# One transpose by DMA for the probabilities of two heads, and the loads of the later batches on GpSimd's queue

## The chip, the cores and the metric

The kernel runs on one core of a Trainium2 chip. The metric is the device time of one execution in microseconds, the median of several runs. The engines are TensorE (PE), VectorE (DVE), ScalarE (ACT), GpSimd (POOL) and SyncE (SP), which here does nothing but issue DMAs; 16 DMA engines move the data for whoever issues.

## The reference

Attention over 4 batches, 12 heads, 448 positions and 64 columns a head, with q and k normalized by rows; its output, 1792 tokens of 768 columns, goes through two expert layers with inner width 2048. All in f32.

```python
q_n, k_n = rmsnorm(q, g_q), rmsnorm(k, g_k)
scores = np.matmul(q_n, k_n.transpose(0, 1, 3, 2)) / np.sqrt(64)
attn = np.exp(scores - scores.max(-1, keepdims=True))
attn = attn / (attn.sum(-1, keepdims=True) + 1e-09)
x = np.matmul(attn, v).transpose(0, 2, 1, 3).reshape(1792, 768)
h = x @ moe_w_in                          # 768 x 2048
y = (h / (1 + np.exp(-1.702 * h))) @ moe_w_out
h = y @ moe2_w_in
out = (np.maximum(h, 0) + moe2_alpha * np.minimum(h, 0)) @ moe2_w_out
```

## The kernel before

**Numbers.** Most factors are split into a high and a low part of 16 bits, and a product is three matmuls (high by high, high by low, low by high) into one f32 sum. To split well, each operand is first scaled by a power of two taken from its largest entry, so that the largest entry of a batch's v has to be known before the batch's v can be split.

**Work.** Heads go in pairs: 24 pairs, six a batch, and a pair has four units: three of 128 rows of both heads and one of 64 rows of both heads, the two heads of which share the 128 partitions. Batch 0 is done in f32 and transposes on PE. For batches 1 to 3 a pair passes through these steps:

- `load_qk` (lines 353 to 356) and `load_v` (368 to 371): four loads for k and q, three for v. There are three buffers for q and k and two for v.
- `normalize`: squares (ACT, line 395), row sums (DVE, 397), reciprocal roots by a seed and three rounds (POOL, 398 to 408, 14 short instructions for two pairs), then the gains and the roots (417, 418). For pairs 8 to 11, the last four of batch 1, POOL also does 417, 418 and the subtraction at 452; otherwise DVE does.
- `prep_pair`: the split of q and k (451, 452), one transpose by DMA of the whole pair (454, a source of 128 x 1792 in f16), the split of v and two copies within SBUF (459, 460).
- for each unit: `scores` (PE, 499; row maxima on DVE, 504, ACT, 506), `exponent` (ACT, 523), `high` (565) and `low` (DVE, 592), which split the normalized probabilities, and the transposes by DMA of line 598, one for each head.
- `values` (PE, 616): the transposed probabilities by v, once for every two units.

`v_scale(b)` finds the largest entry of a batch's v ahead of time: eight pieces of the batch's v are loaded one after another into two buffers (310) and reduced on DVE (311).

**Order.** Attention of batch b+1 is woven into the first expert layer of batch b (`first_moe1`, then `moe1`: lines 720, 767 and 790). The order of the instructions on each engine is planned at build time: an instruction takes the next free slot of its engine on a simulated time line once its inputs and its buffer are there, and the order of the program decides only between those that are ready. So a load without inputs may stand far ahead of its place in the program. Some loads are held back by hand: `tc.issue_after(ins)` lets the instructions of its block that run on the engine of `ins` follow `ins`. It is used for the pieces of v of batch 1 (behind the last load of the first layer's first weights), of batches 2 and 3 (behind the q-and-k transpose of the last pair but one of the batch before), and for the first pairs of batch 1 (behind a load of the first layer's second weights). All three name an instruction of SP. Each engine then works through its list in order; SP issues every DMA of the kernel, and a DMA that must wait for a buffer or for data holds what follows it on SP.

After attention of batch 3 the rest of the first layer and the whole second layer follow (lines 892 and 1052), almost all on PE.

Of the kernel before, what the change touches and what calls it, by code (L numbers as in the profile page):

```python
# [10 lines left out]
F16 = mybir.dt.float16  # L11
# [45 lines left out]
def attention_moe_kernel(  # L57
# [17 lines left out]
    nc = tc.nc  # L75
    B, H, S, D = q.shape
# [60 lines left out]
    def split(dst, src, scale):  # L137

        nc.scalar.activation(out=dst[0], in_=src, func=AF.Copy, scale=scale)  # L139
        nc.vector.scalar_tensor_tensor(  # L140
            out=dst[1], in0=src, scalar=scale, in1=dst[0], op0=ALU.mult, op1=ALU.subtract
        )
# [124 lines left out]
    att_p = att.enter_context(tc.tile_pool(name="att_p", bufs=2))  # L267
# [29 lines left out]
    def v_scales(b, col):  # L297
        one = small.tile([128, 1], F32, tag="vone", name="vone")
        nc.vector.tensor_reduce(out=one, in_=col, op=ALU.max, axis=AX)
        pow2floor(one, one)  # L300
        partition_max(mv[:, b:b + 1], one)
        scaled_reciprocal(av[:, b:b + 1], mv[:, b:b + 1], 2.0 ** 13)

    def v_scale(b):
        flat = v[b].rearrange("h s d -> (h s d)").rearrange("(p n) -> p n", p=128)
        n = flat.shape[1] // VN
        col = small.tile([128, VN], F32, tag="vcol", name="vcol")
        for i in range(VN):
            t = raw_p.tile([128, n], F32, tag="vst", name="vst")
            nc.sync.dma_start(out=t, in_=flat[:, i * n:(i + 1) * n])  # L310
            nc.vector.tensor_reduce(out=col[:, i:i + 1], in_=t, op=ALU.max, axis=AX, apply_absolute_value=True)
        v_scales(b, col)

# [5 lines left out]
    def first_tiles(P):  # L319

        if P < 4:
            part = held[:, HOLD + P * HELD:]
            a = 2 * NT2 * 128
            return (
                part[:, 0:a].bitcast(F32).rearrange("p (i t) -> p i t", t=S),
                part[:, a:HELD].bitcast(F32).rearrange("p (h c d) -> p h c d", h=2, d=D)
            )
        vr = att_p.tile([128, 22 * D], F16, tag="vs", name="v0")
        return (
            att_p.tile([128, 2, S], F32, tag="t1", name="t1"),  # L330
            vr[:, 0:4 * NV * D].bitcast(F32).rearrange("p (h c d) -> p h c d", h=2, d=D)
        )

    HELD = 2 * NT2 * 128 + 4 * NV * D
    ST = S - S % 128


    def main_rows(src, b, p):

        return src[b, 2 * p:2 * p + 2, 0:ST].rearrange("h (p c) d -> p h (c d)", c=3)  # L340

    def some_rows(src, b, p, first, step=1):

        return src[b, 2 * p:2 * p + 2, first:first + 64 * step:step].rearrange("h s d -> s h d")

    def load_qk(P):

        if P >= B * NP:
            return
        b, p = divmod(P, NP)  # L350
        qk = raw_p.tile([128, 2, NT2, D], F32, tag="qk", name="qk", bufs=QKB)
        places = qk.rearrange("p h c d -> p h (c d)")
        nc.sync.dma_start(out=places[:, :, 0:3 * D], in_=main_rows(k, b, p))
        nc.sync.dma_start(out=places[:, :, 4 * D:], in_=main_rows(q, b, p))
        nc.sync.dma_start(out=qk[0:64, :, 3], in_=some_rows(k, b, p, ST))
        nc.sync.dma_start(out=qk[64:128, :, 3], in_=some_rows(q, b, p, ST))
        raws[P] = qk

    def load_v(P):
        if P >= B * NP:  # L360
            return
        b, p = divmod(P, NP)
        if b:
            vr = raw_p.tile([128, 2, NV, D], F32, tag="vr", name="vr")
        else:
            firsts[P] = first_tiles(P)
            vr = firsts[P][1]
        nc.sync.dma_start(out=vr.rearrange("p h c d -> p h (c d)")[:, :, 0:3 * D], in_=main_rows(v, b, p))
        h = 0 if b else 64
        nc.sync.dma_start(out=vr[h:h + 64, :, 3], in_=some_rows(v, b, p, ST))  # L370
        nc.sync.dma_start(out=vr[64 - h:128 - h, :, 3], in_=some_rows(v, b, p, 0, 3))
        rawv[P] = vr

    preps = {}
# [90 lines left out]
    pts = {}  # L465
# [10 lines left out]
    def unit(u):  # L476

        P, r = divmod(u, 4)
        return (P, *UNITS[r])
# [88 lines left out]
    def low(u):  # L568
        P, half, cols, place = unit(u)
        if u < 4 * NP:  # L570
            pr, _ = probs.pop(u)
            n = len(pr)
            if (P, half) not in pts:
                pts[P, half] = att_p.tile([128, NV, 512], F32, tag="pt", name="ptf")
            for h in range(2):
                tp = ps_m.tile([128, 2, n, 128], F32, tag="m", name="tp")
                for c in range(2):
                    o = min(128 * (2 * h + c), S - 128)
                    for i in range(n):
                        nc.tensor.transpose(out=tp[:, c, i], in_=pr[i][:, o:o + 128], identity=identf)  # L580
                d = cols[1] - cols[0]
                to = pts[P, half][:, 2 * h:2 * h + 2, 0:2 * d].rearrange("p c (i t) -> p c i t", i=2)
                to = to[:, :, :, cols[0]:cols[0] + 64 * n]
                src = tp if n == 2 else tp.rearrange("p c n (i t) -> p c (n i) t", i=2)
                nc.scalar.activation(out=to, in_=src, func=AF.Copy)
            if u % 2:
                spread_sums(P, half)
            return
        pr, sm, ph = probs.pop(u)
        n = len(pr)  # L590
        for i in range(n):
            nc.vector.scalar_tensor_tensor(  # L592
                out=ph[:, i, S:2 * S], in0=pr[i], scalar=sm[:, i:i + 1], in1=ph[:, i, 0:S], op0=ALU.mult, op1=ALU.subtract
            )
        if (P, half) not in pts:
            pts[P, half] = att_p.tile([128, 7, 512], F16, tag="pt", name="pt")
        for i in range(2):
            nc.sync.dma_start_transpose(  # L598
                out=pts[P, half][:, :, cols[i]:cols[i] + 64 * n], in_=ph[:, i] if n == 2 else ph[64 * i:64 * i + 64, 0]
            )  # L600

    def values(P, half):
        b, p = divmod(P, NP)
        vs = preps[P][1]
        pt = pts.pop((P, half))
        if half == 0 or b == 0:
            xps[P] = ps_x.tile([128, S], F32, tag="x", name="xp")
        xp = xps[P]
        if b == 0:
            steps = [(c, c, slice(64 if c == 3 else 0, 128)) for c in range(NV)]  # L610
        else:
            steps = [(c, c, slice(0, 128)) for c in range(7)] + [(c + 7, c, slice(0, 128)) for c in range(4)]
        parts = PARTS[half]
        for i, (c, kc, ks) in enumerate(steps):
            for j, o, t, n in parts:
                nc.tensor.matmul(  # L616
                    out=xp[64 * j:64 * j + 64, t:t + n],
                    lhsT=vs[ks, j, c],
                    rhs=pt[ks, kc, o:o + n],
                    start=(i == 0),  # L620
                    stop=(i == len(steps) - 1),
                )
        if b and half == 0:
            xs[b, p] = big.tile([128, 2, S], F16, tag="x", name="x", bufs=NX)
        elif b:
            x = xs[b, p]
            split((x[:, 0], x[:, 1]), xp, scales["w1i"][1][:, p:p + 1])
        elif half == 0:
            own = spread.pop((P, 0))
            nc.vector.tensor_tensor(out=own, in0=xp[:, 0:FIRST], in1=own, op=ALU.mult)  # L630
        else:
            own = spread.pop((P, 1))
            cols = slice(FIRST, S)
            nc.vector.scalar_tensor_tensor(
                out=own, in0=xp[:, cols], scalar=first_sc[:, p:p + 1], in1=own, op0=ALU.mult, op1=ALU.mult
            )
            x = xs[0, p]
            nc.scalar.activation(out=x[:, 0, cols], in_=own, func=AF.Copy)
            nc.vector.tensor_tensor(out=x[:, 1, cols], in0=own, in1=x[:, 0, cols], op=ALU.subtract)
# [504 lines left out]
    if True:  # L1144
        make_identity(nc, ident)
        nc.vector.memset(ones, 1.0)
        nc.vector.tensor_copy(out=identf, in_=ident)
        load_qk(0)
        gains()
        load_v(0)  # L1150
        load_qk(1)
        load_v(1)
# [115 lines left out]
```

## Time and profile before

| | us |
|---|---|
| median of 3 runs | 1183.44 (1181.72 to 1184.11) |
| the profiled execution | 1184.74 |
| its span, first to last instruction | 1183.0 |
| PE busy | 1073.3 (91%) |
| DVE busy | 819.6 (69%) |
| ACT busy | 673.3 (57%) |
| POOL busy | 79.7 (7%) |

Busy shares are means over stages with different limits: the start up to 206 us with batch 0 and the splitting of the weights, batches 1 to 3 of attention from 206 to 652 us, and the rest. Issuing DMAs isn't counted as busy time, so that SP has no row; what its queue does is read from the single issues.

### The profile page before, as it was taken

How to read it: one execution, taken by the hardware profiler on the slowest of the kernel's cores; microseconds unless marked ns; L12 is line 12 of the kernel's file. 1: busy time of each engine (PE TensorE's matmuls, PEld its weight loads, DVE VectorE, ACT ScalarE, POOL GpSimd, SP SyncE). 2: the span in 40 equal slices, each digit the busy share in tenths (PEclk: the TensorE clock that was granted, in tenths of full speed). 3: DMA queues.
4: the chain of work that ended last, by engine and by line, in shares of the span. 5: the costliest groups of instructions: out<-in, count | busy, mean ns of one | idle time of the engine just before them, and what ended most of it. 6: DMA issues, size and time to landing. Idle time of an engine off the chain costs nothing.

```text
span 1183.0 us, 18327 instructions
## 1 busy us (share of the span) xinstructions
PE 1073.3 (91%) x6755; PEld 586.6 (50%) x6755; DVE 819.6 (69%) x1445; ACT 673.3 (57%) x1348; POOL 79.7 (7%) x200
## 2 busy tenths in 40 slices
PE   3468799688789989999998999999999999999998
PEld 1234467554344444545454545544444467666665
DVE  6989999986767886467741868489996322978351
ACT  4667776787767875578742545256555423655220
POOL 2300001442011101100000000000000000000000
PEclk9579799899999999999998999999999999999999
DMA  7944542569888685666553821275624423353111
GB/s 232 266 144 137 150 135 77 113 138 182 160 158 157 136 157 121 122 122 115 93 128 65 307 92 52 99 255 178 224 78 144 142 72 123 99 173 101 34 30 31
DMA packets 256458, 158.06 MB, mean 134 GB/s; under 512 B 177648, under 2 KB 239728, under 8 KB 256368
## 3 DMA queue, kind: packets, MB, share of 16 engines
q1 hardware_dynamic: 256368, 156.89, 50.9%
q8 instruction: 53, 0.87, 0.3%
q14 instruction: 37, 0.30, 0.1%
HBM read 92.22 MB, written 25.69 MB: 100 GB/s over the span
## 4 chain that ended last, share of the span: by engine, by line
PE 32%; DVE 20%; DMA 10%; ACT 10%; issue 5%; SPq 3%; POOL 2%; ACTq 0%; POOLq 0%; DVEq 0%
PE op L1052 16%; PE h L892 7%; PE yp L790 5%; ACT pr L523 3%; DVE ph L592 3%; PE hp L767 3%; DVE nm L504 2%; ACT ph L565 2%; SPq L598 2%; DMA yr<-y_dram 2%; DMA qk<-in_q_dram 1%; DMA pt<-ph 1%; DMA t<-hl 1%; DVE g L140 1%; DMA vst<-in_v_dram 1%
## 5 line engine op out<-in xcount | busy, mean ns | idle before, releaser
L790 PE MATMUL yp<-g,w1o 128*128 128x448 f16 x1152 | 228.2, 355 | 1.9 <-DVE g L140 1.6
L892 PE MATMUL h<-x,w2i 128*128 128x512 f16 (+1 forms) x1152 | 218.9, 352 | 2.7 <-DVE pos L898 1.7
L767 PE MATMUL hp<-x,w1i 128*128 128x448 f16 x864 | 172.1, 356 | 3.7 <-DVE t L776 1.8
L892 PEld LDWEIGHTS <-w2i 128*128 128x128 f16 x1152 | 112.6, 98 | 108.1 <-issue 3.5
L790 PEld LDWEIGHTS <-w1o 128*128 128x128 f16 x1152 | 109.8, 98 | 111.8 <-issue 13.2
L767 PEld LDWEIGHTS <-w1i 128*128 128x128 f16 x864 | 82.8, 99 | 88.2 <-issue 15.7
L592 DVE SCALAR_TENSOR_TENSOR ph<-pr,sm,ph 128x448 f16<-128x448 f32 x126 | 86.9, 717 | 20.2 <-ACT ph L565 19.3
L504 DVE TENSOR_REDUCE nm<-sp 128x2 f32<-128x896 f32 x96 | 92.4, 963 | 0.4 <-PE sp L499 0.4
L523 ACT ACTIVATE pr<-sp,nm,c_s 128x448 f32<-128x448 f32 x126 | 90.0, 717 | 2.8 <-DVE ph L592 1.0
L897 ACT ACTIVATE pos<-h,sign 128x512 f32<-128x512 f32 (+1 forms) x64 | 40.2, 629 | 86.0 <-PE h L892 80.2
L565 ACT ACTIVATE ph<-pr,sm 128x448 f16<-128x448 f32 x126 | 77.8, 659 | 18.3 <-DVE sm L562 15.3
L1052 PEld LDWEIGHTS <-even 128*128 128x128 f16 x672 | 65.7, 98 | 43.4
L898 DVE SCALAR_TENSOR_TENSOR pos<-h,slope,pos 128x512 f32<-128x512 f32 (+1 forms) x64 | 43.4, 680 | 57.9 <-ACT pos L897 57.9
L720 PE MATMUL hp<-x,w1i 128*128 128x256 f16 (+1 forms) x576 | 63.9, 273 | 10.0 <-DVE t L732 4.8
L499 PE MATMUL sp<-t 64*128 64x448 f16 (+1 forms) x432 | 56.2, 365 | 17.0 <-ACT pr L523 17.0
L1052 PEld LDWEIGHTS <-odd 128*128 128x128 f16 x504 | 49.3, 98 | 32.6
L616 PE MATMUL xp<-pt,vs 128*64 128x256 f16 (+1 forms) x792 | 50.2, 271 | 16.6 <-DMA pt<-ph 8.4
L1052 PE MATMUL op<-w2lo,even 128*128 128x384 f16 x384 | 63.4, 326 | 0.0
L720 PEld LDWEIGHTS <-w1i 128*128 128x128 f16 x576 | 54.6, 103 | 17.5 <-issue 12.9
L140 DVE SCALAR_TENSOR_TENSOR g<-t,ratio_w1o,g 128x448 f16<-128x448 f32 x64 | 47.0, 736 | 15.0 <-ACT g L139 14.9
L506 ACT ACTIVATE nm<-nm,c_s 128x2 f32<-128x2 f32 x72 | 20.9, 290 | 62.4 <-DVE nm L504 62.2
L616 PEld LDWEIGHTS <-vs 128*64 128x64 f16 x792 | 39.3, 114 | 33.7 <-issue 18.7
(228 smaller groups left out, 1553.8 us busy)
## 6 DMA issues: line engine op xcount, KB each, us to landing
g<-in_moe_w_in_dram SPq DMA_DIRECT2D x24, 512.0 KB, 5.7
g<-in_moe_w_out_dram SPq DMA_DIRECT2D x32, 384.0 KB, 3.7
w2raw<-in_moe_w_in_dram SPq DMA_DIRECT2D x24, 512.0 KB, 5.6
w2raw<-in_moe_w_out_dram SPq DMA_DIRECT2D x16, 768.0 KB, 6.3
g_dram<-pos SPq DMA_DIRECT2D x48, 256.0 KB, 2.0
gp<-g_dram SPq DMA_DIRECT2D x8, 1024.0 KB, 6.7
odd<-g_dram SPq DMA_DIRECT2D x6, 1024.0 KB, 5.4
y_dram<-y SPq DMA_DIRECT2D x24, 224.0 KB, 2.5
```

Source lines behind the costliest of these rows:

```text
L140: nc.vector.scalar_tensor_tensor(out=dst[1], in0=src, scalar=scale, in1=dst[0], op0=ALU.mult, op1=ALU.subtract)
L499: nc.tensor.matmul(out=sp[:, j, 0:S] if n == 2 else sp[ds, 0, 0:S], lhsT=qt[ds] if n == 2 else qt[ds, 64:128], rhs=kt[ds, 0:S], start=(i = ...
L504: nc.vector.tensor_reduce(out=nm[:, 0:n], in_=sp[:, 0:n, 0:S], op=ALU.max, axis=AX, negate=True)
L523: nc.scalar.activation(out=pr[i], in_=sp[:, i, 0:S], func=AF.Exp, bias=nm[:, i:i + 1], scale=c_s if u >= 4 * NP else 1.0, accum_out=sm[:, ...
L565: nc.scalar.activation(out=ph[:, i, 0:S], in_=pr[i], func=AF.Copy, scale=sm[:, i:i + 1])
L592: nc.vector.scalar_tensor_tensor(out=ph[:, i, S:2 * S], in0=pr[i], scalar=sm[:, i:i + 1], in1=ph[:, i, 0:S], op0=ALU.mult, op1=ALU.subtract)
L616: nc.tensor.matmul(out=xp[64 * j:64 * j + 64, t:t + n], lhsT=vs[ks, j, c], rhs=pt[ks, kc, o:o + n], start=(i == 0), stop=(i == len(steps) ...
L720: nc.tensor.matmul(out=ps, lhsT=w1i[:, kk, e, m * 128:(m + 1) * 128], rhs=xs[0, kk][:, f, cols], start=(i == 0), stop=(i == 3 * KD - 1))
L767: nc.tensor.matmul(out=ps, lhsT=w1i[:, kk, e, m * 128:(m + 1) * 128], rhs=x[:, f], start=(n == 0), stop=(n == 3 * KD - 1))
L790: nc.tensor.matmul(out=ps, lhsT=w1o[:, m, e, j * 128:(j + 1) * 128], rhs=g[:, m, f], start=(n == 0), stop=(n == 3 * KF - 1))
L892: nc.tensor.matmul(out=ps, lhsT=w2i[:, kk, e, m * 128:(m + 1) * 128], rhs=x2[kk][:, f], start=(c == 0), stop=(c == 3 * KD - 1))
L1052: nc.tensor.matmul(out=ps, lhsT=ops[:, o, m, f], rhs=rhs[:, e], start=(c == 0), stop=(c == 3 * KH - 1))
```

## The change

Two edits.

The transposed probabilities of a unit, so far 7 blocks of 512 columns with both heads side by side, become 14 blocks of 256 columns, 7 for each head. For the three units with 128 rows of both heads one transpose of 128 x 1792 takes the place of two of 128 x 896. The unit with 64 rows keeps its two. `values` reads the same number of columns from the new places.

The loads of q, k and v of batches 1 to 3, in `load_qk`, `load_v` and `v_scale`, are issued by GpSimd; those of batch 0, and all other DMAs, stay on SyncE. The uses of `issue_after` aren't touched.

```diff
@@ v_scale
-            nc.sync.dma_start(out=t, in_=flat[:, i * n:(i + 1) * n])
+            nc.gpsimd.dma_start(out=t, in_=flat[:, i * n:(i + 1) * n])
@@ load_qk
-        nc.sync.dma_start(out=places[:, :, 0:3 * D], in_=main_rows(k, b, p))
-        nc.sync.dma_start(out=places[:, :, 4 * D:], in_=main_rows(q, b, p))
-        nc.sync.dma_start(out=qk[0:64, :, 3], in_=some_rows(k, b, p, ST))
-        nc.sync.dma_start(out=qk[64:128, :, 3], in_=some_rows(q, b, p, ST))
+        queue = nc.gpsimd if b else nc.sync
+        queue.dma_start(out=places[:, :, 0:3 * D], in_=main_rows(k, b, p))
+        queue.dma_start(out=places[:, :, 4 * D:], in_=main_rows(q, b, p))
+        queue.dma_start(out=qk[0:64, :, 3], in_=some_rows(k, b, p, ST))
+        queue.dma_start(out=qk[64:128, :, 3], in_=some_rows(q, b, p, ST))
@@ load_v (its three loads in the same way)
@@ low
-            pts[P, half] = att_p.tile([128, 7, 512], F16, tag="pt", name="pt")
-        for i in range(2):
+            pts[P, half] = att_p.tile([128, 14, 256], F16, tag="pt", name="pt")
+        pt = pts[P, half]
+        if n == 2:
             nc.sync.dma_start_transpose(
-                out=pts[P, half][:, :, cols[i]:cols[i] + 64 * n], in_=ph[:, i] if n == 2 else ph[64 * i:64 * i + 64, 0]
+                out=pt[:, :, cols[0]:cols[0] + 128], in_=ph.rearrange("p i k -> p (i k)")
             )
+        else:
+            for i in range(2):
+                nc.sync.dma_start_transpose(out=pt[:, 7 * i:7 * i + 7, 128:192], in_=ph[64 * i:64 * i + 64, 0])
@@ values
-                    rhs=pt[ks, kc, o:o + n],
+                    rhs=pt[ks, 7 * j + kc, 0:n] if b else pt[ks, kc, o:o + n],
```

## Rows read from the trace of the kernel before

**Rows 1.** Stages: stretch, length, busy of the engines, PE clock, DMA share, GB/s.

```profile
0.00:60.00 60.00, 26.85 (x106) 13.13 (x106) 46.59 (x97) 32.28 (x62) 17.97 (x62) 0.77 0.82 248
60.00:180.00 120.00, 97.30 (x641) 56.27 (x640) 107.59 (x239) 87.60 (x195) 0.00 (x0) 0.87 0.49 144
206.00:240.00 34.00, 23.46 (x215) 18.06 (x213) 31.38 (x60) 26.25 (x62) 14.57 (x21) 0.85 0.60 123
240.00:345.00 105.00, 88.62 (x672) 45.78 (x672) 77.14 (x142) 77.36 (x192) 23.82 (x43) 0.98 0.79 159
345.00:440.00 95.00, 86.83 (x594) 43.60 (x593) 77.60 (x135) 73.34 (x168) 10.86 (x34) 0.96 0.80 155
652.00:1183.00 531.00, 521.98 (x2923) 285.64 (x2921) 340.13 (x534) 232.71 (x347) 0.00 (x0) 1.00 0.37 124
```

**Rows 2.** Waits of PE from 240 to 440 us: total, times, longest.

```profile
PE sp L499 <- ACT pr L523: 11.1, 8, 3.4
PE xp L616 <- DMA pt<-ph: 7.8, 5, 2.7
```

**Rows 3.** Waits of DVE in the same stretch, the longest.

```profile
DVE vcol L311 <- DMA vst<-in_v_dram: 12.3, 8, 3.6
```

**Rows 4.** The chain of waits from 240 to 440 us, by line.

```profile
by line: DVE ph L592 7.9%; issue 7.6%; DMA pt<-ph 7.6%; DMA vst<-in_v_dram 7.0%; DVE nm L504 6.4%; SPq L598 6.0%; DMA t<-hl 5.4%; ACT pr L523 4.6%; DMA qk<-in_q_dram 4.4%; DVE ss L397 3.5%; ACT ph L565 3.1%; DVE g L140 2.7%; DVE qk L418 2.3
```

**Rows 5.** Transposes of the probabilities: issue in ns (min/median/max), and flight.

```profile
L598 SPq DMA_TRANSPOSE pt<-ph x144: 1187/1250/2723, 225.1 to 639.6; - x144
...
DMA to landing us min/median/max: 2.5/3.0/6.5
```

**Rows 6.** Transposes of q and k: issue, first and last start, and flight.

```profile
L454 SPq DMA_TRANSPOSE t<-hl x18: 1391/1607/2592, 206.4 to 570.1; - x18
...
DMA to landing us min/median/max: 3.9/4.3/5.6
```

**Rows 7.** Loads of q, k, v and pieces of v: issue.

```profile
L353 SPq DMA_DIRECT2D qk<-in_k_dram x24: 368/559/1477, 0.7 to 488.6; - x24
L354 SPq DMA_DIRECT2D qk<-in_q_dram x24: 367/468/940, 1.2 to 489.2; - x24
L355 SPq DMA_DIRECT2D qk<-in_k_dram x24: 604/630/1217, 1.7 to 490.3; - x24
L356 SPq DMA_DIRECT2D qk<-in_q_dram x24: 595/605/685, 2.5 to 490.9; - x24
...
L368 SPq DMA_DIRECT2D vr<-in_v_dram x18: 374/546/1377, 37.2 to 554.9; - x18
L370 SPq DMA_DIRECT2D vr<-in_v_dram x18: 601/635/663, 37.9 to 555.5; - x18
L371 SPq DMA_DIRECT2D vr<-in_v_dram x18: 601/618/835, 38.6 to 556.2; - x18
...
L310 SPq DMA_DIRECT2D vst<-in_v_dram x24: 327/422/1046, 78.1 to 433.7; - x24
```

**Rows 8.** SyncE's issues from 285 to 291 us: start, length, instruction, count.

```profile
285.83 0.92 SPq L310 DMA_DIRECT2D vst<-in_v_dram  x2
...
287.33 2.58 SPq L598 DMA_TRANSPOSE pt<-ph  x2
290.02 1.00 SPq L310 DMA_DIRECT2D vst<-in_v_dram  x2
```

**Rows 9.** SyncE's issues from 0 to 200 us, two of them.

```profile
37.18 0.37 SPq L368 DMA_DIRECT2D vr<-in_v_dram  x1
...
41.80 0.59 SPq L822 DMA_DIRECT2D slope<-in_moe_alpha_dram  x1
```

**Rows 10.** Reductions of the pieces of v: ns, first and last start.

```profile
L311 DVE TENSOR_REDUCE vcol<-vst x24: 470/496/504, 86.7 to 436.6; 128x1 f32<-128x336 f32 x24
```

**Rows 11.** 206 to 262 us: all engines, and POOL's longest operation.

```profile
206.00:262.00 56.00, 43.69 (x388) 30.37 (x386) 51.81 (x94) 44.36 (x106) 29.06 (x39) 0.91 0.65 134
...
L452 POOL TENSOR_TENSOR hl<-qk,hl 128x896 f16<-128x896 f32 x3 | 6.5, 2175 | 7.4 <-ACT hl L451 7.4
```

More of the change, by code (lines that the diff above doesn't have):

```diff
@@ L367, in load_v @@
             vr = firsts[P][1]
-        nc.sync.dma_start(out=vr.rearrange("p h c d -> p h (c d)")[:, :, 0:3 * D], in_=main_rows(v, b, p))
+        queue = nc.gpsimd if b else nc.sync
+        queue.dma_start(out=vr.rearrange("p h c d -> p h (c d)")[:, :, 0:3 * D], in_=main_rows(v, b, p))
         h = 0 if b else 64
-        nc.sync.dma_start(out=vr[h:h + 64, :, 3], in_=some_rows(v, b, p, ST))
-        nc.sync.dma_start(out=vr[64 - h:128 - h, :, 3], in_=some_rows(v, b, p, 0, 3))
+        queue.dma_start(out=vr[h:h + 64, :, 3], in_=some_rows(v, b, p, ST))
+        queue.dma_start(out=vr[64 - h:128 - h, :, 3], in_=some_rows(v, b, p, 0, 3))
         rawv[P] = vr
```

## The prediction

> **What bounds the kernel now.** I read four views in this order: busy time by stage, the waits of the engines in the stage that has room, the chain of waits there, and then the issues of SyncE's queue. The profiled execution took 1184.74 us, 1.74 us more than its span of 1183.0 us, and 1.30 us more than the median of the runs (1183.44 us). All sums are made against 1184.74 and end 1.30 lower.
>
> The table by stage [rows 1] says where time can be had. From 652 us on PE is busy 521.98 of 531 us: nothing that the change touches lives there, but whatever PE gains or loses earlier moves this block as a whole. The change acts on 240 to 440 us, where batches 1 and 2 go through attention while the expert matmuls of the batch before fill PE. PE is busy 88.62 of 105 us and 86.83 of 95 us there, so it stands 16.38 + 8.17 = 24.55 us. That is the most this stretch can give. No arithmetic engine is full in it: DVE 77.14 of 105 and 77.60 of 95 us, ACT about the same. The DMA engines are at 0.79 and 0.80 of their time, nearer to full than DVE.
>
> What PE waits for [rows 2]: 11.1 us for the exponentials that free a score buffer (ACT, line 523) and 7.8 us for the transposed probabilities. The first wait has a cause one engine further back: DVE stands 12.3 us, in eight stalls, for pieces of v that only serve the scale of the next batch [rows 3]. DVE works in order, and behind the stalled reduction stand the row maxima of the scores, which ACT and then PE need. The chain of waits in the same stretch [rows 4] agrees: transposes in flight 7.6%, v pieces in flight 7.0%, the issuing of transposes 6.0%, q in flight 4.4%, together 25% of 200 us, or 50 us that hang on SyncE's queue and its transfers. Shortening them does not give 50 us, since the next chain is close behind; PE's 24.55 us is the bound.
>
> **SyncE's queue.** A transpose of one head's probabilities takes the queue 1.250 us and lands 3.0 us after issue [rows 5]. The transpose of a pair's q and k takes 1.607 us and lands after 4.3 us [rows 6]. The loads take 0.4 to 0.6 us each [rows 7]. Pairs pass at (570.1 - 206.4) / 17 = 21.4 us each, from the first and last start of the 18 q-and-k transposes [rows 6]. Per pair the queue issues 8 x 1.250 + 1.607 + (0.559 + 0.468 + 0.630 + 0.605) + (0.546 + 0.635 + 0.618) = 15.7 us, and in 240 to 440 us, 9.3 pairs, also 16 pieces of v at 0.422, 0.7 a pair. That is 16.4 of 21.4 us, or 77%, before the small copies and stores. It is in order too: two pieces of v are issued at 285.83, the next two only at 290.02, with two transposes (2.58 us) between [rows 8]; DVE stalls there.
>
> **The change, part by part.** *The merged transpose.* 18 pairs have three units each with two heads of 128 rows: 54 units go from two issues to one. The fourth unit (64 rows) keeps two. The trace has no such merged transpose, so its issue lies between 1.250 us (as one now) and 2.500 us (as two). The q-and-k transpose has the same source, 128 x 1792 in f16, so I take its 1.607: 54 x 0.89 = 48 us less issuing, 2.7 us a pair. In landing it gives nothing: two issues end at 1.25 + 3.0 = 4.25 us, the long one at 4.3. It also waits for both heads' low halves where the first transpose could start after one; behind it in the queue stand the copies of v's split halves, the next q-and-k transpose and the stores of the layer's output, none of which PE waits for within a unit. The 792 matmuls that read the result keep their widths, and the tile its bytes: nothing.
>
> *The loads.* 18 pairs x 7 + 3 x 8 = 150 loads leave SyncE: 18 x (2.262 + 1.799) + 24 x 0.422 = 83 us of its queue. With both parts a pair costs it 3 x 1.607 + 2 x 1.250 + 1.607 = 8.9 us of 21.4, under half. A transpose no longer stands behind a load that waits for its buffer, nor a load behind transposes.
>
> *What that is worth.* Of the 7.8 us for probabilities I take 5: the turn in the queue goes, the flight stays. Of the 11.1 us for exponentials I take half, 5.5, because the 12.3 us of DVE stalls feed only part of these waits. Gain 10.5 us; bounds 0 and 24.55.
>
> *What it costs on POOL.* No load is issued by POOL in this trace. From below its issue costs what SyncE's does, about 0.56 us; from above I take POOL's longest operation, 2.175 us [rows 11]. I take 1.0, nearer the lower, since issuing is not a pass over 896 columns. POOL is idle most of the span, but not from 206 to 262 us, where it scales whole pairs: 29.06 of 56 us. By SyncE's order some 22 loads fall there. At 1.0 they fit into the 27 us left; at 2.175 they exceed them by 21 us. The reciprocal roots of q and k stand in the same queue, so each load ahead of them delays the pair; the stage from 206 to 240 us has PE at 23.46 of 34 us and no cover. I take 2 us, bounds 0 and 21.
>
> *What it costs at the start.* The pieces of v for batches 1 to 3 stand in blocks whose order is tied to SyncE instructions. A tie to SyncE does not bind an instruction on POOL, so nothing but two buffers holds these loads. How early that may be is seen in two loads that nothing holds now: v of batch 1 goes out at 37.18 us and the slopes of the second layer at 41.80 us, though the program names them long after [rows 9]. The 16 reductions of batches 2 and 3, at 0.496 us [rows 10], then come into the first 180 us: 7.9 us of DVE, which is busy 46.59 of 60 and 107.59 of 120 us there, and 2 x 1.376 MB (12 x 448 x 64 x 4 bytes a batch), 11 us at the 248 GB/s of the first 60 us. They can fall into DVE's 25 us of gaps. I take 2 us, bounds 0 and 7.9 + 11 = 18.9. On the other side, the same move takes the eight stalls out of 240 to 440; that gain is in the 5.5 above.
>
> Sum: 1184.74 - 10.5 + 2 + 2 = 1178.2; less 1.30, **1177 us**.
>
> **A rule that speaks against it.** SyncE's own time on a load is 0.56 us against a flight of about 3 us for a transpose [rows 5, 7], which looks small, but at 77% and more of a pair the queue is a resource of its own. The Trainium skill (DMA: Bandwidth & Descriptors, "Issuing engines are not separate DMA queues") says that all issuers feed the same 16 DMA engines and that using several saves only the sequencer's time, usually small beside the transfer; by that rule the sum would stay at 1183, and the trace bears it out as far as the DMA share of 0.8 goes. The same page ("Latency and other measured facts") gives about 1 us to the first byte for GpSimd's path against about 0.6 for SyncE's; as an estimate, 0.4 us on each of some eight normalizations would make the sum 1180. No trace of this case shows that.
>
> **The rivals.**
>
> 1. *Hidden.* The queue was full, but flights set the pace: DMA engines at 0.79 to 0.80, the merged flight as long as the two. For it: 4.3 against 4.25 us. Against it: the stalls of DVE end with loads that were issued late. Gain 4 instead of 10.5, costs 4: 1183 us, no change. The rule above is this rival.
>
> 2. *Slower at the start.* The freed pieces of v crowd the first 180 us. If every reduction is paid in DVE time and the loads push the weights of the first layer back by their 11 us, 18.9 us are lost against 10.5 gained: 1183.4 + 8.4 = 1192 us. It decides for slower once the start loses over 10.5 us. For it: DVE at 90% from 60 to 180 us [rows 1]. Against it: gaps of 13 us before 60 and 12 after.
>
> 3. *POOL in order.* A load that waits for its buffer on POOL holds the roots behind it, as SyncE's loads held transposes. It decides for slower where POOL's delays pass 10.5 us; with 15 us of the 21 above it gives 1183.4 - 10.5 + 15 = 1188 us. For it: POOL at 29.06 of 56 us at the batch's start. Against it: it idles for most of the rest.
>
> The change may also not do what it says, if the order planned for all engines comes out different; I give that 2 in 100, at the old time.
>
> **Numbers.** Forecast 0.55, hidden 0.13, start 0.17, POOL 0.13, no effect 0.02. The hidden case has its edge on either side of the 0.2% (2.4 us) that a measurement of this kernel can tell from no change; I count 0.01 of it as faster: faster 0.56, same 0.14, slower 0.30. The forecast's own range is 1168 (15 us net, six tenths of the 24.55 us) to 1181 (just past the 0.2%). For 8 in 10 the range must take in both slower rivals and the full bound: 1162 to 1196.
>
> **What would show it.** Right: 90 probability transposes on SyncE with the merged ones near 1.6 us; DVE's wait for v pieces in 240 to 440 gone; PE's waits there at half; the block after 652 as long as now but starting some 6 us sooner. Wrong: reductions of all three batches before 180 us with DVE's other work later; POOL full at the start of batch 1 and PE idle longer from 206 to 240; or PE's waits for probabilities unchanged with the queue half empty. The forecast falls if issuing on POOL costs near 2 us, or if the merged transpose takes the queue for as long as two.

## The result and the profile after

The change takes 1173.83 us (median of 6 runs, 1171.89 to 1178.25) against 1183.45 us for the kernel before, measured beside it: a ratio of 0.9918, with a 95% interval of 0.9901 to 0.9934, 0.8% faster. The forecast of 1177 us has the right sign and size. Where the time came from is another matter, and the experiments are mostly about that. The profiled execution of the change is the slowest of its six, 1178.25 us, with a span of 1176.5 us, so the traces show 6.5 of the 9.6 us between the medians.

First the issues. The first fence has the transposes and loads of the change by line: duration in ns (min/median/max), first and last start, and under a transpose its flight. They answer to [rows 5, 7, 10].

```profile
L601 SPq DMA_TRANSPOSE pt<-ph x54: 1296/1537/4425, 231.9 to 629.6; - x54
...
DMA to landing us min/median/max: 3.9/4.2/9.6
...
L606 SPq DMA_TRANSPOSE pt<-ph x36: 1189/1266/2570, 248.0 to 634.8; - x36
...
L310 POOL DMA_DIRECT2D vst<-in_v_dram x24: 536/556/792, 6.1 to 111.3; - x24
...
L354 POOL DMA_DIRECT2D qk<-in_k_dram x18: 728/734/793, 56.6 to 484.3; - x18
...
L370 POOL DMA_DIRECT2D vr<-in_v_dram x18: 712/755/862, 1.3 to 553.4; - x18
...
L373 POOL DMA_DIRECT2D vr<-in_v_dram x18: 597/597/606, 2.8 to 554.7; - x18
...
L311 DVE TENSOR_REDUCE vcol<-vst x24: 481/492/503, 15.8 to 114.6; 128x1 f32<-128x336 f32 x24
```

There are 54 merged transposes (L601, two heads) and 36 single ones (L606, the 64-row units). A merged one costs SyncE 1.537 us instead of 2 x 1.250 and lands after 4.2 us. A load costs GpSimd 0.56 to 0.76 us. All 24 pieces of v, for three batches, are out by 111.3 us; before, they went from 78.1 to 433.7 us.

Then the stages, in the form of [rows 1], with finer ones after 500 us:

```profile
206.00:240.00 34.00, 22.66 (x220) 17.89 (x218) 29.88 (x60) 23.62 (x53) 22.74 (x39) 0.88 0.39 82
240.00:345.00 105.00, 90.86 (x711) 50.82 (x710) 82.05 (x144) 80.47 (x196) 52.88 (x88) 0.94 0.85 162
345.00:440.00 95.00, 86.45 (x605) 43.61 (x600) 71.63 (x120) 73.88 (x173) 31.17 (x60) 0.98 0.80 138
...
500.00:512.00 12.00, 12.00 (x85) 6.07 (x84) 6.80 (x12) 6.90 (x17) 1.98 (x3) 1.00 0.86 152
512.00:520.00 8.00, 8.00 (x62) 4.02 (x61) 5.16 (x8) 6.11 (x16) 0.00 (x0) 1.00 0.30 65
...
620.00:640.00 20.00, 18.10 (x112) 9.75 (x110) 4.85 (x10) 7.21 (x17) 0.00 (x0) 1.00 0.42 96
```

The same finer stages of the kernel before, which the rows ahead of the prediction do not have:

```profile
500.00:512.00 12.00, 10.15 (x58) 4.66 (x53) 8.01 (x12) 6.97 (x17) 0.00 (x0) 0.95 0.62 125
512.00:520.00 8.00, 8.00 (x55) 3.90 (x52) 4.82 (x9) 5.54 (x13) 0.00 (x0) 0.86 0.55 118
...
620.00:640.00 20.00, 14.67 (x86) 8.27 (x85) 5.36 (x11) 6.58 (x16) 0.00 (x0) 0.84 0.32 65
```

From 240 to 440 us, where the prediction put the gain, PE stands 14.14 + 8.55 = 22.69 us instead of 24.55, and the clock is lower in the first half (0.94 for 0.98) and higher in the second (0.98 for 0.96). These are the same microseconds and not the same work, since the change comes late into them (below); the table of moments further down sets that right. Two more places show a gain, and the prediction does not name them. At 500 to 520 us PE stood 1.85 us before, and the granted clock was 0.95 and 0.86 there; in the change it neither stands nor slows. At 620 to 640 us it stood 5.33 us with the clock at 0.84, now 1.90 us at 1.00.

PE's waits from 240 to 440 us, to be read against [rows 2], and DVE's longest wait there, against [rows 3]:

```profile
PE sp L501 <- ACT pr L525: 9.7, 8, 2.7
PE xp L622 <- DMA pt<-ph: 6.7, 4, 3.5
PE hp L726 <- DVE t L738: 6.5, 2, 3.6
```

```profile
DVE ss L399 <- ACT sq L397: 12.5, 5, 6.0
```

DVE's 12.3 us of waits for pieces of v are gone. But DVE's longest wait in total is now 12.5 us for the squares of ACT that start the roots, PE's two waits fell by 1.4 and 1.1 us only, and the wait for DVE's output in the first layer, 6.5 us, is now as long as that for probabilities.

The start lost time. The next fence is GpSimd's timeline in the change; each row has start, length, operation, and in brackets the idle time before it with its releaser.

```profile
5.49 0.61 POOL L373 DMA_DIRECT2D vr<-in_v_dram  x1 [0.46 <-issue]
6.09 1.12 POOL L310 DMA_DIRECT2D vst<-in_v_dram  x2
10.81 0.26 POOL L400 TENSOR_SCALAR ss<-ss 128x14 f32<-128x14 f32 x1 [3.61 <-DVE ss L399]
...
16.00 0.26 POOL L400 TENSOR_SCALAR ss<-ss 128x14 f32<-128x14 f32 x1 [3.75 <-DVE ss L399]
16.21 0.22 POOL L410 TENSOR_TENSOR rs<-tn,rs 128x14 f32<-128x14 f32 x1
16.74 0.61 POOL L310 DMA_DIRECT2D vst<-in_v_dram  x1 [0.30 <-DVE vcol L311]
```

The roots of pair 0 (L403 to L410) are not finished when GpSimd's list comes to pair 1's first operation, the second L400. That one waits 3.75 us, and pair 0's chain goes on behind it until 22 us, with two pieces of v and steps of pair 1 between its own. PE's first transpose of q starts at 23.51 us instead of 14.99:

```profile
23.51 0.90 PE L441 MATMUL qt<-identf,qn 128*128 128x128 f32 x3 [10.13 <-DVE qn L434]
```

Batch 1's first scores then start at 219.60 us instead of 210.90. The change starts 8.7 us late and still wins, which needs explaining.

### The profile page after: what moved, and what is told of

It is laid out like the page before. It is cut to its first block, busy times and chain, and to the rows that moved or that the text cites. A ratio compares the mean times of both kernels' runs of the same rounds, so it can differ in the third digit from the quotient of the medians.

```text
span 1176.5 us, 18337 instructions
## 1 busy us (share of the span) xinstructions
PE 1064.7 (91%) x6755; PEld 586.5 (50%) x6755; DVE 818.7 (70%) x1445; ACT 671.9 (57%) x1348; POOL 178.1 (15%) x350
## 3 DMA queue, kind: packets, MB, share of 16 engines
q0 software_dynamic: 6912, 17.11, 6.0%
## 4 chain that ended last, share of the span: by engine, by line
PE 38%; DVE 21%; DMA 14%; ACT 13%; issue 8%; POOL 5%; SPq 1%; ACTq 0%; DVEq 0%; POOLq 0%
PE op L1058 16%; PE h L898 10%; PE yp L796 5%; ACT pr L525 4%; DMA qk<-in_q_dram 4%; DVE nm L506 3%; PE hp L773 3%; PE hp L726 2%; DVE ph L594 2%; ACT ph L567 2%; DMA g<-in_moe_w_out_dram 2%; DMA yr<-y_dram 1%; DMA t<-hl 1%; DMA w2raw<-in_moe_w_in_dram 1%; DMA g<-in_moe_w_in_dram 1%
## 5 line engine op out<-in xcount | busy, mean ns | idle before, releaser
L726 PE MATMUL hp<-x,w1i 128*128 128x256 f16 (+1 forms) x576 | 66.5, 279 | 11.3 <-DVE t L738 7.8
L140 DVE SCALAR_TENSOR_TENSOR g<-t,ratio_w1o,g 128x448 f16<-128x448 f32 x64 | 44.7, 705 | 18.4 <-ACT g L139 18.0
L622 PE MATMUL xp<-pt,vs 128*64 128x256 f16 (+1 forms) x792 | 47.2, 265 | 8.8 <-DMA pt<-ph 6.7
L139 ACT ACTIVATE g<-t,ratio_w1o 128x448 f16<-128x448 f32 x64 | 42.0, 664 | 20.8 <-DVE t L782 18.6
```

Source lines behind the costliest of these rows:

```text
L140: nc.vector.scalar_tensor_tensor(out=dst[1], in0=src, scalar=scale, in1=dst[0], op0=ALU.mult, op1=ALU.subtract)
L622: nc.tensor.matmul(out=xp[64 * j:64 * j + 64, t:t + n], lhsT=vs[ks, j, c], rhs=pt[ks, 7 * j + kc, 0:n] if b else pt[ks, kc, o:o + n], star ...
L726: nc.tensor.matmul(out=ps, lhsT=w1i[:, kk, e, m * 128:(m + 1) * 128], rhs=xs[0, kk][:, f, cols], start=(i == 0), stop=(i == 3 * KD - 1))
```

## The experiments

M is the merged transpose, L the loads of q, k and v on GpSimd, P the pieces of v on GpSimd; the change is M, L and P. Every ratio is to the kernel before, measured beside it; its medians were 1186.63 us (e1 to e4), 1187.29 (e5 to e8), 1186.06 (e9 to e11) and 1184.40 (e12).

### One or two parts

**e1: M alone**, as an edit of the change:

```diff
-            nc.gpsimd.dma_start(out=t, in_=flat[:, i * n:(i + 1) * n])
+            nc.sync.dma_start(out=t, in_=flat[:, i * n:(i + 1) * n])
...
-        queue.dma_start(out=places[:, :, 0:3 * D], in_=main_rows(k, b, p))
+        nc.sync.dma_start(out=places[:, :, 0:3 * D], in_=main_rows(k, b, p))
...
```

> The merged transposes alone; all loads stay on SyncE. Theory (SyncE's queue and the stalls behind it are what the change relieves, and the crowded start is what it pays): 48 us of issuing go, no start cost, but the eight stalls of DVE for v pieces stay; 3 to 6 us faster than before, about 1179. Rival (the loads are all of the gain, since a merged transpose lands no earlier): 1183, no change.

1186.31 us, ratio 0.9994 (0.9975 to 1.0012). Nothing: the rival was right.

**e2: L alone**, as an edit of the kernel before:

```diff
+        queue = nc.gpsimd if b else nc.sync
-        nc.sync.dma_start(out=places[:, :, 0:3 * D], in_=main_rows(k, b, p))
+        queue.dma_start(out=places[:, :, 0:3 * D], in_=main_rows(k, b, p))
...
```

> The loads of q, k and v alone on GpSimd; two transposes a unit, v pieces on SyncE with their holds. Theory: 73 us of issuing leave SyncE, and the v pieces wait less in the queue; 4 to 8 us faster, about 1177, with only part of the late start (first output matmul of layer one at some 252 us). Rival (POOL in order holds the roots at the start of batch 1): slower than 1183, PE idle longer from 206 to 240 us.

1186.48 us, ratio 0.9996 (0.9979 to 1.0014). Nothing; it was neither faster, as the theory had it, nor slower, as the rival had it.

**e3: P alone**, as an edit of the kernel before:

```diff
-            nc.sync.dma_start(out=t, in_=flat[:, i * n:(i + 1) * n])
+            nc.gpsimd.dma_start(out=t, in_=flat[:, i * n:(i + 1) * n])
```

> The v pieces alone on GpSimd. Theory: the 12.3 us of DVE stalls from 240 to 440 us go, but the 16 reductions come before 200 us and the first output matmul of layer one comes some 8 us later than 249 us; the sum is near nothing, 1180 to 1186. Rival (the pieces are the main gain of the change): 1176 or less.

1189.81 us, ratio 1.0032 (1.0012 to 1.0051), slower. The theory's "near nothing" comes closer than the rival. GpSimd's timeline has a load that waits for its buffer with the roots of pair 0 behind it:

```profile
18.72 0.56 POOL L310 DMA_DIRECT2D vst<-in_v_dram  x1 [3.99 <-DVE vcol L311]
```

PE's first transpose of q starts at 26.31 us here (25.47 in e5), and at 16.97 and 17.95 us in e2 and e4, which have the loads on GpSimd and not the pieces. So the late start comes with the pieces.

**e4: M and L**, as an edit of the change:

```diff
-            nc.gpsimd.dma_start(out=t, in_=flat[:, i * n:(i + 1) * n])
+            nc.sync.dma_start(out=t, in_=flat[:, i * n:(i + 1) * n])
```

> The change without the move of the v pieces, which stay on SyncE with their holds. Theory: the first output matmul of layer one comes back from 261 to about 252 us, the DVE stalls for v pieces return in part; as fast as the change or faster, 1168 to 1174. Rival (the early v pieces are worth more than they cost): slower than the change, 1177 or more.

1187.78 us, ratio 1.0017 (0.9996 to 1.0038). The theory fell and the rival was right: the early pieces, which seemed to be the change's one loss, are a part it can't do without. In this kernel DVE's waits for pieces are still 8.6 us (200 to 440 us).

**e5: M and P**, the change with the loads (`queue`) on SyncE, as in e1.

> The change without its second part: merged transposes and the pieces of v on GpSimd, the loads of q, k and v on SyncE. Theory (the three parts pay only together, because each alone leaves one of two queues late: SyncE's with the loads, or VectorE's with the v pieces): the pieces of batches 1 to 3 are over by some 110 us, VectorE's waits for them between 240 and 440 us (7 to 9 us in the kernels with the pieces on SyncE) go, and the merged transposes take some 50 us of issuing from SyncE, so most of the change's gain is there: 1177 to 1182 us, ratio 0.992 to 0.997. Rival (the gain of the change comes from its planned order as a whole, not from a queue): within 0.3% of before, 1183 to 1190 us, as with the four kernels that do one or two parts so far.

1185.07 us, ratio 0.9977 (0.9966 to 0.9989): a quarter of a per cent, and not most of the gain. That is what the rival's bounds say; its reason, the order, is not shown by it.

**e6: L and P**, as an edit of the change:

```diff
-            pts[P, half] = att_p.tile([128, 14, 256], F16, tag="pt", name="pt")
-        pt = pts[P, half]
-        if n == 2:
+            pts[P, half] = att_p.tile([128, 7, 512], F16, tag="pt", name="pt")
+        for i in range(2):
             nc.sync.dma_start_transpose(
...
```

> The change without its first part: two transposes for a unit, all loads of q, k, v for later batches and the pieces of v on GpSimd. Theory (the merged transpose shortens the chain from the probabilities to the values, which is the part that the other two cannot give): within 0.2% of before or slower, 1184 to 1191 us, since it pays the 7 to 9 us at the start and keeps the longer chain at the end of attention. Rival (SyncE's queue is relieved enough by the loads, and VectorE's waits for the pieces are gone): as good as the change, ratio 0.990 to 0.995.

1178.64 us, ratio 0.9934 (0.9918 to 0.9949). The rival was right: all of the change's gain is there without its first part.

**e7: the change with the pieces held back.** The two ties of the pieces (`issue_after`) name an instruction of SyncE; here they name loads that GpSimd issues.

```diff
...
-        queue.dma_start(out=qk[64:128, :, 3], in_=some_rows(q, b, p, ST))
+        qk_loads[P] = queue.dma_start(out=qk[64:128, :, 3], in_=some_rows(q, b, p, ST))
...
-                    with tc.issue_after(moved[P].ins):
+                    with tc.issue_after(qk_loads[P + 2].ins):
                         v_scale(P // NP + 1)
...
-                with tc.issue_after(loads["w1i"][-1].ins):
+                with tc.issue_after(qk_loads[NP + 1].ins):
                     v_scale(1)
```

> The change, with the pieces of v still issued by GpSimd, but those of batch 1 held until the first batch-1 loads of q and k are issued and those of batches 2 and 3 until loads of q and k two pairs ahead are issued, instead of all in the first 115 us. Theory (the change loses 7 to 12 us at its start to the early pieces, which delay GpSimd's root chain of the first pair and VectorE): the first transposes on TensorE begin near 15 us again instead of 23.5, batch 1's first scores near 211 instead of 219.6 us, and the time is 4 to 9 us below the change's own, 1169 to 1175 us. Rival (early pieces are what keeps VectorE free later, and the start's loss is made up anyway): no faster than the change, with VectorE's waits for the pieces back between 240 and 440 us.

**e8: the change again**, beside e5 to e7.

> The change itself once more, beside the three kernels above on their chip. Theory (the gain is the change's): ratio to before 0.990 to 0.994 again. Rival (part of the gain belongs to the chip or the day): ratio above 0.996, and then the experiments with one and two parts were no worse than the change there.

e7: 1181.97 us, ratio 0.9948 (0.9928 to 0.9967). e8: 1180.73 us, ratio 0.9949 (0.9937 to 0.9961). e8 meets neither expectation: the gain is 0.5% here for 0.8% at first, and the two intervals don't meet. e7 gets back the start (first transpose of q at 17.11 us for 23.16 in e8, batch 1's scores at 212.51 for 221.07) and is no faster. Its reductions, and what DVE waits for from 200 to 440 us:

```profile
L311 DVE TENSOR_REDUCE vcol<-vst x24: 475/494/505, 81.8 to 391.0; 128x1 f32<-128x336 f32 x24
```

```profile
DVE vcol L311 <- DMA vst<-in_v_dram: 9.8, 3, 4.3
```

The stalls are back, 9.8 us for the 8.6 us won at the start, and from batch 1's first scores to the first layer's first matmul for batch 2 e7 takes 296.2 us where e8 takes 288.2. Early pieces and stalled DVE are two prices for the same reductions.

### How much is the planned order?

Every edit gives every engine another order. e9 to e11 measure that by itself: the kernels before, of the change, and of e6, each with a useless memset of one column on GpSimd.

```diff
-        nc.vector.memset(ones, 1.0)
+        nc.vector.memset(ones, 1.0); nc.gpsimd.memset(small.tile([128, 1], F32, tag="nil", name="nil", bufs=1), 0.0)
```

> The kernel before with one memset of one column on GpSimd at the very start, which no result uses: its own work is under 0.1 us, but the build plans the order of every engine anew from there. It tells how much of a difference between kernels is the planned order alone. Theory (the change's gain is its queues'; an order like another costs nothing): within 0.2% of before. Rival (every build has an order of its own that is worth some tenths of a per cent either way): 0.3 to 0.8% off, in either direction, at places where the profile has stalls of a few microseconds.

> The change with the same useless memset. Theory: as good as the change, ratio to before 0.992 to 0.996. Rival (the change's gain is its order's): the gain goes for a half or more, ratio above 0.997, or grows as much.

> The change without its merged transposes (loads and pieces of v on GpSimd), with the same useless memset. Theory (loads and pieces together are what pays, whatever the order): ratio to before 0.991 to 0.996 as without the memset. Rival: above 0.997.

e9: 1183.64 us, ratio 0.9983 (0.9970 to 0.9996). e10: 1179.18 us, 0.9945 (0.9928 to 0.9962). e11: 1179.97 us, 0.9956 (0.9939 to 0.9972). e9's theory and those of e10 and e11 held. Another order alone is worth about 0.2% here (0.9983 for 1, 0.9956 for 0.9934), and the change in one and the same order gave 0.9918 and 0.9949, 0.3% apart. So 0.2% between two of these kernels measured side by side means nothing, nor does 0.3% between two measured apart, and what holds in both orders is the change's.

All of it together, with four moments from PE's timelines: the first scores of batch 1, the first layer's first matmul for batch 2, that layer's second product for batch 2, and its first matmul for batch 3, in us.

```
              parts       ratio    scores 1   first 2   second 2   first 3
before        -           1         210.90     504.76     582.42    654.65
e9            - nil       0.9983    208.81     500.27     577.10    651.99
e1            M           0.9994    210.56     507.97     585.01    656.60
e2            L           0.9996    204.18     509.02     585.65    659.77
e3            P           1.0032    217.87     512.42     588.74    661.98
e4            M L         1.0017    208.31     512.77     589.23    659.64
e5            M P         0.9977    216.06     507.88     585.29    656.50
e6            L P         0.9934    220.93     501.28     577.65    650.52
e11           L P nil     0.9956    222.77     504.34     578.56    650.34
change        M L P       0.9918    219.60     506.51     580.37    647.47
e8            M L P       0.9949    221.07     509.22     583.02    650.01
e10           M L P nil   0.9945    222.02     504.32     578.13    645.86
e7            M L P held  0.9948    212.51     508.75     582.55    649.98
e12           L P no trip 0.9902    220.09     500.41     576.85    641.98
```

Three things are to be read here. (In e2 and e4 "scores 1" comes some 54 matmuls earlier in PE's work than in the others, so that their column is not like the rest.) The six kernels with L and P and free pieces start batch 1's scores last, some 10 us after the kernel before, and yet reach "first 2" at 500 to 509 us, where e1 to e5 reach it at 508 to 513. No kernel that lacks L or P is below 0.9977. And from "second 2" to "first 3" the kernels with all three parts take 67.0 to 67.7 us, those with L and P but two transposes 71.8 and 72.9, the two orders of the kernel before 72.2 and 74.9.

The moments also cut the profile into stretches of the same work. First the kernel before, then the change, in the form of [rows 1]:

```profile
0.00:210.90 210.90, 153.19 (x1038) 94.39 (x1039) 182.03 (x396) 137.83 (x291) 22.13 (x76) 0.86 0.56 163
210.90:504.76 293.86, 258.01 (x1851) 135.25 (x1851) 218.89 (x382) 212.59 (x502) 57.58 (x124) 0.97 0.73 144
504.76:582.42 77.66, 75.81 (x528) 37.68 (x526) 54.17 (x92) 62.04 (x144) 0.00 (x0) 0.98 0.66 117
582.42:654.65 72.23, 66.90 (x435) 35.00 (x434) 24.40 (x41) 28.35 (x68) 0.00 (x0) 0.95 0.44 100
```

```profile
0.00:219.60 219.60, 150.83 (x1038) 95.77 (x1039) 189.04 (x419) 138.44 (x290) 54.73 (x128) 0.88 0.58 170
219.60:506.51 286.91, 255.66 (x1851) 135.54 (x1851) 212.26 (x362) 213.31 (x508) 117.52 (x213) 0.96 0.75 138
506.51:580.37 73.86, 73.86 (x527) 37.31 (x526) 52.29 (x90) 58.54 (x135) 5.83 (x9) 1.00 0.62 117
580.37:647.47 67.10, 65.20 (x436) 33.84 (x435) 24.86 (x42) 29.19 (x70) 0.00 (x0) 1.00 0.49 107
```

From "scores 1" to "first 2", 1851 matmuls in both, the change is 7.0 us shorter, and PE stands 31.25 us instead of 35.85. In the same stretch PE stands 22.4 to 30.6 us in the other five kernels with L and P and free pieces, which are 5.7 to 13.5 us shorter than the kernel before. It stands 33.9 to 39.2 us in e9, e1, e3, e5 and e7, which take 291.5 to 297.4 us.

### The stretch where the merged transpose pays

e10 and e11 are the pair to compare, since they reach "second 2" at 578.13 and 578.56 us. SyncE, DVE and PE in e11 (two transposes), from their timelines:

```profile
608.64 2.56 SPq L600 DMA_TRANSPOSE pt<-ph  x2
611.30 0.53 SPq L127 DMA_DIRECT2D line<-yone  x1
618.93 0.32 SPq L128 DMA_DIRECT2D row<-line  x1
...
623.89 0.29 DVE L133 TENSOR_REDUCE my<-row 128x1 f32<-128x128 f32 x1 [9.98 <-DMA row<-line]
...
632.23 0.68 DVE L140 SCALAR_TENSOR_TENSOR x<-xp,ratio_w1i,x 128x448 f16<-128x448 f32 x1 [1.15 <-ACT x L139]
...
632.96 2.56 PE L618 MATMUL xp<-pt,vs 128*64 128x256 f16 x22 [5.29 <-DVE x L140]
```

and the same in e10 (merged):

```profile
607.57 0.32 SPq L127 DMA_DIRECT2D line<-yone  x1
608.20 1.49 SPq L601 DMA_TRANSPOSE pt<-ph  x1
615.34 0.33 SPq L128 DMA_DIRECT2D row<-line  x1
...
621.17 0.29 DVE L133 TENSOR_REDUCE my<-row 128x1 f32<-128x128 f32 x1 [9.88 <-DMA row<-line]
...
629.03 0.68 DVE L140 SCALAR_TENSOR_TENSOR x<-xp,ratio_w1i,x 128x448 f16<-128x448 f32 x1 [1.14 <-ACT x L139]
...
629.77 1.39 PE L622 MATMUL xp<-pt,vs 128*64 128x256 f16 x22 [2.53 <-DVE x L140]
```

The second layer's first block needs the maximum of |y| over all partitions. It is found by a trip: a column is written to DRAM (line) and read back as a row. DVE works in order and stands 10 us for the row, with the last units' probabilities behind it, and then the split of x (L140) that frees the buffer of PE's product with v. In e11 two transposes stand in SyncE's queue ahead of the column, 2.56 us; in e10 they do not. The column goes 3.7 us sooner, x is done 3.2 us sooner, and PE stands 2.53 us instead of 5.29. After the longer stand the same 22 matmuls take 2.56 us instead of 1.39: the granted clock from 630 to 640 us is 0.83 in e11, a mean of its two levels (1.2 and 2.4 GHz), and 1.00, the upper level, in e10.

The other traces bear this out. In all six kernels with the trip and two transposes a unit (both orders of the kernel before, e2, e3, e6, e11) two transposes stand right ahead of the column, and PE then stands 5.3 to 8.1 us. In all seven with M the column goes ahead of the merged transpose, and PE stands 3.1 to 3.9 us in e1, e4 and e5 and 1.8 to 2.5 us in the four with all three parts.

**e12: L and P without the trip**, as an edit of e6; the maximum is found on TensorE, as the later blocks do.

```diff
-        if i == 0:
-            row = send_max(one)
-            yield
-            take_max(my, row)
-        else:
-            yield
-            partition_max(my, one)
+        yield
+        partition_max(my, one)
```

> Loads of q, k, v and the pieces of v on GpSimd, two transposes for a unit, and the maximum over the partitions that the second layer's first block needs found on TensorE (one 128x128 product) instead of by a column written to DRAM and read back as a row. Theory (the last stall of attention, TensorE's wait of 5.5 us near 630 us and the clock of 0.66 behind it, comes from that trip: VectorE waits 10.3 us for the row with the last units' probabilities behind it; the merged transposes, where they pay, pay there, so without the trip two transposes lose nothing): VectorE's wait for the row is gone, TensorE's wait near 630 us is under 2 us with the clock at 1.00, and the time is 4 to 7 us below the 1178.6 to 1180.0 us of the two kernels without merged transposes, 1172 to 1176 us, ratio 0.988 to 0.991. Rival (the trip is hidden, the stall comes from the two transposes' issue on SyncE): the stall stays at 5 us or more, ratio 0.993 to 0.996.

1172.94 us, ratio 0.9902 (0.9881 to 0.9923), and the theory held in each of its numbers. DVE, PE and the stages near 630 us:

```profile
619.62 0.68 DVE L140 SCALAR_TENSOR_TENSOR x<-xp,ratio_w1i,x 128x448 f16<-128x448 f32 x1 [1.14 <-ACT x L139]
...
625.89 1.39 PE L618 MATMUL xp<-pt,vs 128*64 128x256 f16 x22
```

```profile
620.00:630.00 10.00, 10.00 (x69) 5.47 (x68) 1.05 (x3) 1.30 (x2) 0.00 (x0) 1.00 0.35 70
630.00:640.00 10.00, 10.00 (x71) 5.40 (x69) 0.68 (x1) 1.27 (x2) 0.00 (x0) 1.00 0.18 47
```

x is done at 620.3 us, 12 us sooner, PE never stands, and the clock stays at 1.00. "Second 2" to "first 3" falls to 65.1 us, below that of the kernels with merged transposes. This is the version with the lowest ratio of the study; its interval meets that of the change's first measurement (0.9901 to 0.9934) and lies below the ones of e8 and e10. It was built in one order only; M without the trip was not built.

## Why the prediction was right, and where not

**The bound.** Right. From the first layer's first matmul for batch 3 to the end of the span the kernel before takes 1183.0 - 654.65 = 528.4 us, the change 1176.5 - 647.47 = 529.0. What PE gained, it gained earlier; the block starts 7.2 us sooner (forecast: some 6).

**The queue.** Right in every size: 1.537 us an issue for 1.607 taken, a landing of 4.2 us for 4.3, 54 units, 150 loads off SyncE.

**What that is worth** was mis-sized, and less than it looks. 5 us of PE's wait for probabilities and 5.5 of that for exponentials were to come back between 240 and 440 us; 1.1 and 1.4 did, and PE's standing time there fell by 1.9 us where 10.5 was taken. But the change comes into these 200 us some 9 us late. Over the same work, from "scores 1" to "first 2", it gains 7.0 us, 4.6 of them standing, and the other kernels with L and P and free pieces 5.7 to 13.5. That is not the late start alone: e3 starts 7.0 us late and takes 294.6 us there, no less than the kernel before. So the gain was in the right place and two thirds of its size in the change. What failed is the reason given for half of it: a queue at 77% was read as a queue that sets the pace. e1, e2 and e4 relieve it in three ways and gain nothing, so for the queue by itself the rival "hidden" holds. The Trainium skill (DMA: Bandwidth & Descriptors, "Issuing engines are not separate DMA queues") says that several issuers save only the sequencer's time, usually small beside the transfer, and the ratios of 0.9996 (e2) and, beside 0.9994 for M alone, 1.0017 (e4) agree. Where the pieces are on GpSimd too, moving the loads takes 4.3 us off (e5 to e8, measured side by side); whether that is issuing time is not shown. The trip near 610 us is the exception in this trace, where 2.56 us of issuing stand ahead of a 10 us wait.

**DVE's stalls** went, as forecast, in every kernel with P and free pieces. By themselves (e3) they bring nothing over the whole kernel, and held back (e7) they cost in attention what they save at the start; with the loads on GpSimd too (e6, e11) they go with a gain of 0.4 to 0.7%. I take it that L alone still has 7.9 us of these stalls (e2), and that P alone pays the late start and still has the loads among the transposes. The table fits that, but it was argued and not shown; that L and P pay only together is shown by the table, and why stays open.

**GpSimd.** An issue took 0.56 to 0.76 us for 1.0 taken: so its price at batch 1's start, 2 us, was not too small. PE had 22.66 us from 206 to 240 us for 23.46, at a slightly higher clock (0.88 for 0.85). What a load takes to land did change: from 200 us on, the main load of k lands 4.0 us after its issue by GpSimd and 2.8 after SyncE's.

```profile
L353 SPq DMA_DIRECT2D qk<-in_k_dram x16: 376/576/1477, 204.5 to 488.6; - x16
...
DMA to landing us min/median/max: 2.5/2.8/3.6
```

```profile
L354 POOL DMA_DIRECT2D qk<-in_k_dram x16: 728/732/793, 212.5 to 484.3; - x16
...
DMA to landing us min/median/max: 2.8/4.0/8.3
```

The prediction's estimate of 0.4 us more was too low for these loads. What the 1.2 us cost the kernel was not measured.

**The start** is the mis-sized term: 2 us taken, 8.5 us at PE's first transpose of q, 8.7 at batch 1's first scores. The rival "slower at the start" was right on the loss and wrong on its mechanism: the roots of pair 0 wait on GpSimd in order, behind another pair's and among the pieces. That is the mechanism of the rival "POOL in order", at batch 0 and not at batch 1, where the prediction looked for it. The rival "slower at the start" was also wrong on its end, since the loss is made up again. By "first 2" the change stands at 506.51 us for 504.76, and e7, without that loss, is at 508.75 and no faster than e8.

**The sum** was right to 3 us by luck in its parts. At "first 2" the change is 1.8 us behind, 8.7 lost and 7.0 won. What it wins comes after that, in a stretch to which the prediction gave nothing: 3.8 us between "first 2" and "second 2" (73.9 for 77.7) and 5.1 us from there to "first 3" (67.1 for 72.2). The second of these is the merged transpose at the trip, 3.4 us of standing and 1.7 us by the clock that did not fall. The prediction put the merged transpose at nothing beyond the queue, since PE waits within a unit for none of what stands behind it, and did not count the column, for which PE does wait. The 3.8 us are half standing, the stand at 508 us that the change is spared, and half clock (0.98 and 1.00); all four kernels with M, L and P and e11 are spared it, e6 and e12 are not (1.4 and 1.5 us of standing from 500 to 520), so it hangs on the order too. The other order of the kernel before takes 76.8 us there, with the clock at 1.00. Over the whole kernel the merged transpose can't be told from none: 0.9949 for 0.9934 and 0.9945 for 0.9956. In the first of these pairs it is 7.9 us behind at "first 2", in the second level with it; why is open.

## What to carry to other kernels

Price a wait by what stands behind it and by what its removal costs elsewhere: DVE's stalls for pieces of v were worth some 8 us to PE in attention (e7 against e8) and cost as much at the start, while one wait of 10 us with the bottleneck's buffer behind it was worth 0.3 to 0.5% (e12 against e6 and e11, measured apart). Compare two traces between the same points of the work: the same 200 us showed 1.9 us of the change's gain, the same 1851 matmuls 7.0. A tie between instructions binds only on the queue that it names, so a load that moves to another queue goes out at once unless its tie moves with it. Where a build plans its own order, measure that order's spread with an edit that does nothing, and trust a part's effect only if it shows in two orders.

## What the runs showed of the hardware

A stand of 5.3 us on TensorE cost more than itself: the 22 matmuls behind it took 2.56 us for 1.39 (e11), and the granted clock from 630 to 640 us was 0.83. After a stand of 2.5 us (e10) they took 1.39 us at 1.00. Over all kernels with the trip they took 2.51 to 2.56 us after stands of 3.1 to 8.1 us and 1.39 after stands of 1.8 to 2.5 us.

A load issued by GpSimd cost that engine 0.56 to 0.76 us, somewhat more than SyncE's 0.42 to 0.64 for the same loads [rows 7], and the main load of k landed 1.2 us later after its issue. One transpose of 128 x 1792 took 1.54 us of SyncE where two of 128 x 896 take 2.50.
